# Sixteen parts of unread products of ones, placed in TensorE's order by new tables

## The chip, the cores and the metric

The kernel runs on one core of one Trainium2 chip. A time is the device time of one execution in microseconds; the median of several is compared. The core's engines each play an own queue of instructions in order and meet through semaphores: TensorE (PE, matmuls; its weight loads are PEld), VectorE (DVE), ScalarE (ACT) and GpSimd (POOL). SyncE (SP) starts DMAs. Matmul results stand in eight PSUM banks, the rest in SBUF.

## The reference

Eight batches of eight heads, 576 positions of 64 numbers. The attention is causal by blocks of 64 positions, and its result is the input of a mixing layer of width 512.

```python
scores = q @ k.T / 8, masked where block(key) > block(query)     # blocks of 64
x      = softmax(scores) @ v                       # (8, 576, 512): 8 heads side by side
theta  = x @ w_theta
zr, zi = x * cos(theta), x * sin(theta)
y      = w_tok_r @ zr + w_tok_i @ zi               # over the 576 positions
u      = x + y
out    = u + maximum(u @ w_ch, 0)
```

## The kernel before

The work is cut into 3434 parts, small functions that each issue one to some tens of instructions, mostly on one engine. 64 heads go in 32 pairs (one head in each half of the partitions), eight heads make a batch of the mixing layer.

For a pair, SyncE loads q, k and v. The first pairs use them in f32; later ones are split into a high and a low f16 part (`q_high`, `k_high`, then the lower parts at L581 and L586), with scales from the maxima of the data (L395 spreads them over the partitions by a product with ones, from a diagonal made at L382 on VectorE, L387 on ScalarE or L389 on GpSimd). Scores (L610, mask L617, the first small tile L638) come in wide tiles, which take two banks each (`s_123`, `s_124` in the order), and narrow ones in single banks (`g_125` to `g_128`). VectorE takes row maxima (L658), someone turns them into a bias (L668 or L670), ScalarE makes the exponentials (L674, tiles `t_110`, `t_111`). The first eight heads are transposed by TensorE (L699) and copied out of the banks (L450 ScalarE, L452 VectorE or GpSimd); the others are split into f16 parts (high L450/L452, low L455) and transposed by a DMA (L721). Then come the weighted sums (L732, f32, the first four heads, L741 in f16) and their division by the row sums (L757 to L765).

The mixing layer makes theta (L888, six or nine matmuls a step), its sines (to L931), the products with x (L940), their f16 parts (low L455), the mixing over positions (L964), u = x + y (the copy of x, L969; the sum, L973), its f16 parts, the last product (L987), the rectifying pass (L993 ScalarE, L995 VectorE) and the sum (L1003).

The weights come in raw by DMA (L481) and are rounded and split: an exponent on ScalarE (L490), the lowest bits (L496 ScalarE, L498 GpSimd, L500 VectorE), a narrowing on VectorE (L504), then the plain part (L459 or L520). Their column sizes come from products with ones (L513). Ahead of all, `WARMING = 11` matmuls of 128x512 ones with ones (L363) run while the first data are loaded.

No engine's order follows from the code alone. `emit` plays the parts in the order of a table, and so sets every engine's queue:

```python
for label in parts[key].takes:
    of_label[label] = banks[int(next(names))]          # BANKS: a digit for each label
if parts[key].on:
    place[key] = next(places, parts[key].on[0])        # PLACES: A, D, P or S
...
for n in ORDER:                                        # numbers of parts
    parts[keys[n]].f(*([place[keys[n]]] if parts[keys[n]].on else []))
```

`ORDER` holds each part once, `BANKS` the bank of each tile of results, `PLACES` the engine of each part that several can do (A ScalarE, D VectorE, P GpSimd, S SyncE). The waits follow from what a part reads and writes.

Of the kernel before, what the change touches and what calls it, by code (L numbers as in the profile page):

```python
# [37 lines left out]
WARMING = 11  # L38
WHOLE = 3

ORDER = [
# [214 lines left out]
def attention_phase_mixer(  # L256
# [10 lines left out]
    nc = tc.nc  # L267
# [927 lines left out]
    for b, m in enumerate(mixers):  # L1195
# [45 lines left out]
        for e, th in mixes:  # L1241
# [4 lines left out]
            part("out", (e, th), m.total, [("relu", b, e, th), ("ul", b, e)], leaves=[("c", b, e, th)])  # L1246
        for e in range(NDT):
            part("store", (e,), m.store, [("out", b, e, th) for th in range(2)])

    with tc.manual_schedule():  # L1250
        emit(parts, banks, bank_of)

# [45 lines left out]
```

## Time and profile before

| | us |
|---|---|
| median of 3 runs | 644.75 (644.53 to 645.04) |
| the profiled execution | 644.28 |
| its span | 642.5 |
| TensorE busy | 617.8 |
| VectorE, ScalarE, GpSimd busy | 566.7, 521.1, 358.5 |

The span runs from the first to the last instruction of the profiled execution. In the rows below `DVE`, `ACT`, `POOL`, `PE` name the engines, and `L610` is line 610 of the kernel before. A matmul's busy time is modelled by its end, so starts are the surer numbers.

### The profile page before, as it was taken

To read this page: it belongs to the slowest core of one execution; us is meant where nothing else is said; L and a number is where in the kernel's file an instruction comes from. 1 tells how busy PE (TensorE), PEld (TensorE's weight loads), DVE (VectorE), ACT (ScalarE), POOL (GpSimd) and SP (SyncE) were. 2 spreads that over 40 slices of the span, in tenths; PEclk is the share of its full clock that TensorE was granted. 3 is DMA by queue.
4 is the path that set the end of the run, shared out by engine and by line. 5 is a ranking of instruction groups with operands and counts; after the bars stand their busy time and mean duration, and the time that the engine had idled before them with its cause. 6 is when DMAs were issued, how large, how long until landed. Compare 5 with 4: busy or idle time off the path is not lost.

```text
span 642.5 us, 18107 instructions
## 1 busy us (share of the span) xinstructions
PE 617.8 (96%) x7423; PEld 467.6 (73%) x7425; DVE 566.7 (88%) x1129; ACT 521.1 (81%) x869; POOL 358.5 (56%) x383
## 2 busy tenths in 40 slices
PE   6899989999999999999999999999999999999997
PEld 3778657866886678767878678785876678857775
DVE  5899999888989999999999989899999989777654
ACT  5899899988997999889999999979998998127112
POOL 3436586673744548448695377572656563734340
PEclk8999999999999999999999999999999999999999
DMA  8964998999696797979799996979796647920101
GB/s 321 387 244 134 162 209 175 206 188 245 104 254 134 158 213 179 196 155 193 147 215 181 174 195 184 192 128 238 192 217 134 124 90 137 183 60 2 38 38 74
DMA packets 238772, 109.23 MB, mean 170 GB/s; under 512 B 226017, under 2 KB 226017, under 8 KB 238689
## 3 DMA queue, kind: packets, MB, share of 16 engines
q1 hardware_dynamic: 238688, 108.07, 76.6%
q8 instruction: 58, 0.95, 0.6%
q14 instruction: 26, 0.20, 0.1%
HBM read 42.01 MB, written 9.44 MB: 80 GB/s over the span
## 4 chain that ended last, share of the span: by engine, by line
PE 61%; ACT 18%; DVE 11%; issue 5%; DMA 3%; POOL 2%; SPq 1%; DVEq 0%; ACTq 0%; POOLq 0%
PE g L964 14%; PE s L964 8%; PE g L741 7%; PE g L888 5%; PE s L888 5%; ACT t L674 5%; PE g L987 5%; PE s L610 5%; PE s L987 4%; DVE m L658 3%; ACT aa L931 2%; PE g L610 2%; ACT junk L850 2%; DMA rk<-in_k 1%; ACT rr L929 1%
## 5 line engine op out<-in xcount | busy, mean ns | idle before, releaser
L964 PEld LDWEIGHTS <-zh 128*128 128x128 f16 x1152 | 112.7, 98 | 31.9 <-issue 2.6
L455 POOL TENSOR_TENSOR p<-t,p 128x1536 f16<-128x1536 f32 (+4 forms) x28 | 75.7, 2706 | 72.9 <-ACT p L450 41.1
L964 PE MATMUL g<-wT_h,zh 128*128 128x288 f16 x378 | 108.4, 287 | 0.2 <-DVE rr L906 0.2
L964 PE MATMUL g<-wT_l,zh 128*128 128x288 f16 x378 | 108.2, 286 | 0.0
L964 PE MATMUL g<-wT_h,zl 128*128 128x288 f16 x378 | 108.2, 286 | 0.0
L741 PEld LDWEIGHTS <-pt 128*128 128x128 f16 x2700 | 89.8, 98 | 8.8 <-issue 2.8
L741 PE MATMUL g<-v,pt 128*128 128x65 f16 x2700 | 92.5, 194 | 3.5 <-DVE xn L765 1.3
L658 DVE TENSOR_REDUCE m<-s 128x1 f32<-128x448 f32 (+2 forms) x132 | 85.0, 671 | 5.0 <-PE s L617 4.8
L450 ACT CAST p<-t 128x1536 f16<-128x1536 f32 (+4 forms) x51 | 68.1, 1337 | 0.9
L964 PEld LDWEIGHTS <-zl 128*128 128x128 f16 x576 | 56.3, 98 | 16.0 <-issue 1.5
L888 PEld LDWEIGHTS <-xT 128*128 128x128 f16 x384 | 36.6, 98 | 41.4 <-issue 1.9
L455 DVE TENSOR_TENSOR p<-t,p 128x1600 f16<-128x1600 f32 (+4 forms) x36 | 61.6, 1715 | 4.6 <-ACT p L450 3.9
L674 ACT ACTIVATE t<-s,m,size 128x576 f32<-128x576 f32 (+1 forms) x80 | 60.1, 779 | 6.5 <-DVE m L670 2.5
L658 DVE TENSOR_REDUCE m<-g 128x1 f32<-128x192 f32 (+2 forms) x156 | 54.3, 370 | 7.4 <-PE g L617 7.4
L964 PE MATMUL s<-wT_h,zh 128*128 128x288 f16 x198 | 56.7, 286 | 1.0 <-ACT t L674 1.0
L987 PEld LDWEIGHTS <-wch_h 128*128 128x128 f16 x512 | 48.2, 98 | 12.5 <-issue 0.2
L964 PE MATMUL s<-wT_h,zl 128*128 128x288 f16 x198 | 56.7, 286 | 0.0
L964 PE MATMUL s<-wT_l,zh 128*128 128x288 f16 x198 | 56.7, 286 | 0.0
L674 ACT ACTIVATE t<-g,m,size 128x320 f32<-128x320 f32 (+2 forms) x100 | 50.2, 534 | 1.3 <-POOL m L670 0.8
L940 POOL TENSOR_TENSOR aa<-aa,xn 128x256 f32<-128x256 f32 (+1 forms) x59 | 46.4, 798 | 8.8 <-ACT aa L931 7.0
L987 PE MATMUL g<-uh,wch_h 128*128 128x288 f16 x152 | 43.6, 287 | 0.1
L987 PE MATMUL g<-uh,wch_l 128*128 128x288 f16 x152 | 43.5, 286 | 0.0
(208 smaller groups left out, 1640.9 us busy)
## 6 DMA issues: line engine op xcount, KB each, us to landing
rv<-in_v SPq DMA_DIRECT2D x16, 768.0 KB, 5.8
rq<-in_q SPq DMA_DIRECT2D x15, 640.0 KB, 5.3
out<-xT SPq DMA_DIRECT2D x32, 288.0 KB, 2.6
rk<-in_k SPq DMA_DIRECT2D x15, 576.0 KB, 4.6
w_raw<-in_w_tok SPq DMA_DIRECT2D x5, 576.0 KB, 5.8
pt<-in_w_tok SPq DMA_DIRECT2D x4, 576.0 KB, 9.1
w_raw<-in_w_theta SPq DMA_DIRECT2D x4, 512.0 KB, 7.6
w_raw<-in_w_ch SPq DMA_DIRECT2D x4, 512.0 KB, 4.2
```

What stands on the lines that cost most here:

```text
L450: nc.scalar.copy(out=out, in_=x)
L455: engine_of(on).tensor_tensor(out=out, in0=x, in1=y, op=ALU.subtract)
L610: nc.tensor.matmul(to[hh][:, col:col + n], lhsT=qq[rows, P + P * i:P + P * i + P], rhs=kk[rows, k0:k0 + n], start=nn == 0 and col % 512 == ...
L658: nc.vector.tensor_reduce(out=self.m[:, i:i + 1], in_=self.scores_of(i), axis=AX.X, op=ALU.max)
L674: nc.scalar.activation(out=t_parts[self.hh][:, to:to + n], in_=self.scores_of(i), func=AF.Exp, scale=self.scales()[0], bias=self.m[:, NI + ...
L741: nc.tensor.matmul(o[:, i, :], lhsT=source[:, block, :], rhs=vv[:, slot, hh, :], start=first, stop=last)
L850: nc.scalar.activation(out=junk[:, 0:PG * n].rearrange("p (g c) -> p g c", g=PG), in_=x, func=AF.Abs, accum_out=self.scales_of(what, g).su ...
L888: nc.tensor.matmul(g, lhsT=xT[:, xx + i, :], rhs=ww[:, dt, :], start=first, stop=last)
L931: nc.scalar.activation(out=to, in_=x, func=AF.Sin, scale=-2.0 * math.pi, bias=half_pi[rows])
L940: engine_of(on).tensor_tensor(out=cd, in0=cd, in1=self.xns[dt][:, i0:i0 + ni, :], op=ALU.mult)
L964: nc.tensor.matmul(g, lhsT=zz[:, kk, cols], rhs=ww[:, kk, ts], start=(n == 0 and kk == k0 and nn == 0), stop=n == 4 and kk == k0 + ni - 1 ...
L987: nc.tensor.matmul(g[:, 0:HS], lhsT=ww[:, dt, e * P:(e + 1) * P], rhs=uu[:, dt, th * HS:(th + 1) * HS], start=dt == 0 and n == 0, stop=dt ...
```

## The change

`FILLS = 16` new parts are added, 3450 in all. Each is two matmuls of 128x512 of the tile `ones` with itself into a bank that the tables name; no instruction reads the result. They come in order of their number. All three tables are new: the order of all parts, the bank of all tiles, the engine of all parts with a choice. No other function is changed. Lines of the kernel after stand two lower down to the new function (L363 becomes L365).

```diff
+FILLS = 16
...
 ORDER = [
-    157, 154, 0, 16, 8, 32, 40, 324, 155, 352, 323, 328, 158, 1, 353, 24, 329, 2, 340, 360, 325, 327, 351, 361, 9, 17,
...
 BANKS = (
-    "6516655545201236420123455012346501235420123650123100123540123640123540123460123560123560123560123450123540123540"
+    "6536423445101236520123455012346501235410123650123100123540123640123540123460123560123560123560123450123540123540"
...
+    def fill(n):
+
+        for _ in range(2):
+            nc.tensor.matmul(bank_of["f", n], lhsT=ones, rhs=ones.unsqueeze(1).broadcast_to([P, 4, P]), start=True, stop=True)
+
+    for n in range(FILLS):
+        add(("fill", n), step_of(fill, n), [("fill", n - 1) for _ in range(n > 0)], takes=[("f", n)])
```

TensorE at the front, from the mask of the first wide scores on. Before, with transposes of the first narrow exponentials (`t_111`) and then the second pair's narrow scores:

```order
L617 LDWEIGHTS mask_q
L617 MATMUL s_124<-ones,mask_q 128x2x64
L638 MATMUL g_128<-rk,rq 128x64
L699 MATMUL g_125<-ident_r,t_111 128x128 x4
L610 MATMUL g_125<-rk,rq 128x320
L610 MATMUL g_126<-rk,rq 128x320
```

And after:

```order
L619 MATMUL s_124<-ones,mask_q 128x2x64
L1255 LDWEIGHTS ones
L1255 MATMUL g_125<-ones 128x512
L1255 LDWEIGHTS ones
L1255 MATMUL g_125<-ones 128x512
L701 MATMUL g_126<-ident_r,t_111 128x128 x4
L701 MATMUL g_127<-ident_r,t_110 128x128 x4
L612 MATMUL g_125<-rk,rq 128x320
```

Fill 0 stands behind the first wide scores, and the transposes of both heads (`t_111`, `t_110`) ahead of the second pair's scores; before, those of `t_110` stood behind them.

VectorE at the front, from its third instruction on. Before, row maxima of the first narrow scores come first:

```order
L321 CAST ident_r<-made_ident 128x128
L658 TENSOR_REDUCE m<-g_125 128x1
L658 TENSOR_REDUCE m<-g_127 128x1
L658 TENSOR_REDUCE m<-g_125 128x1
L658 TENSOR_REDUCE m<-g_127 128x1
L670 TENSOR_SCALAR m<-m 128x2
```

And after:

```order
L323 CAST ident_r<-made_ident 128x128
L506 SCALAR_TENSOR_TENSOR w_val<-w_val,w_raw 128x512
L502 TENSOR_SCALAR w_raw<-w_raw 128x512
L660 TENSOR_REDUCE m<-g_127 128x1
L660 TENSOR_REDUCE m<-g_126 128x1 x2
L660 TENSOR_REDUCE m<-g_127 128x1
```

A narrowing and the lowest bits of two pieces of theta stand ahead of the same four maxima. On SyncE the start of the first piece of theta stands ahead of those of the first q and k, which were the first two before.

TensorE among the transposes ahead of the narrow scores that started at 50 us before (`t_110`, `t_111` are exponentials, `g` and `s` banks). Before:

```order
L732 MATMUL g_128<-qk_103,pt_120 128x65 x15
L699 MATMUL s_123<-ident_r,t_110 128x128 x8
L699 MATMUL g_126<-ident_r,t_110 128x128
L699 MATMUL s_124<-ident_r,t_111 128x128 x8
L610 MATMUL g_126<-rk,rq 128x320
```

And after:

```order
L701 MATMUL s_123<-ident_r,t_110 128x128 x8
L1255 LDWEIGHTS ones
L1255 MATMUL g_126<-ones 128x512
L1255 LDWEIGHTS ones
L1255 MATMUL g_126<-ones 128x512
L701 MATMUL g_126<-ident_r,t_110 128x128
L701 MATMUL s_124<-ident_r,t_111 128x128 x8
L1255 LDWEIGHTS ones
L1255 MATMUL g_125<-ones 128x512
```

Fills 5 and 6 stand between the same transposes, and fill 7 follows a few rows on. The places of all: 0 and 1 ahead of the second wide scores, 2 to 4 from there to the third, 5 to 7 here, 8 ahead of narrow scores that ran at 88 us before, 9 to 13 in one row ahead of a weighted sum (L743) and 14 and 15 ahead of scores, both between 89 and 106 us.

On the other engines: VectorE makes 21 copies of x (L969) in place of 14, GpSimd 11 in place of 18. VectorE makes the low part of 10 tiles of 1536 exponentials (L455) in place of 7, GpSimd 14 in place of 17. VectorE makes 10 low parts of 512 cosines in place of 15, 25 products of `rr` (L940) in place of 31. Half of a head's copy to the other partitions (`other_half`) is a DMA 5 times in place of 14.

## Rows read from the trace of the kernel before

**Rows 1.** The page: busy time, share and instructions; granted clock in 40 slices.

```profile
PE 617.8 (96%) x7423; PEld 467.6 (73%) x7425; DVE 566.7 (88%) x1129; ACT 521.1 (81%) x869; POOL 358.5 (56%) x383
...
PEclk8999999999999999999999999999999999999999
```

**Rows 2.** Stretches: us from:to, length, busy us (and instructions) of each engine, clock, DMA.

```profile
5.60:23.57 17.97, 11.46 (x79) 8.53 (x80) 13.86 (x30) 13.93 (x27) 5.06 (x8) 0.81 1.00 394
23.57:41.45 17.88, 16.03 (x137) 14.23 (x138) 17.24 (x42) 16.59 (x29) 6.42 (x9) 1.00 0.79 296
41.45:88.98 47.53, 47.19 (x547) 36.28 (x547) 45.95 (x102) 42.41 (x83) 31.01 (x40) 1.00 0.74 175
88.98:106.40 17.42, 13.47 (x202) 10.27 (x203) 16.60 (x38) 16.94 (x29) 12.62 (x16) 1.00 0.87 185
106.40:134.00 27.60, 27.60 (x371) 22.71 (x368) 25.35 (x61) 26.62 (x51) 18.83 (x19) 1.00 1.04 196
...
141.60:527.30 385.70, 380.04 (x4891) 283.88 (x4888) 359.99 (x703) 353.69 (x570) 230.87 (x219) 1.00 0.85 177
527.30:638.40 111.10, 111.08 (x1109) 85.80 (x1108) 79.10 (x144) 43.70 (x74) 43.96 (x40) 1.00 0.38 77
```

**Rows 3.** TensorE's timeline: start, us, line, tiles, and in brackets the wait before.

```profile
12.63 1.12 PE L699 MATMUL g<-ident_r,t 128*128 128x128 f32 x4 [3.40 <-ACT t L674]
15.12 2.18 PE L610 MATMUL g<-rk,rq 64*128 64x320 f32 x12 [1.38 <-DMA rk<-in_k]
...
23.57 2.19 PE L610 MATMUL s<-rk,rq 64*128 64x512 f32 x14 [0.63 <-DVE pt L452]
```

**Rows 4.** The front on VectorE and ScalarE, the same columns.

```profile
6.90 1.42 DVE L658 TENSOR_REDUCE m<-g 128x1 f32<-128x320 f32 x4 [4.48 <-PE g L617]
...
8.11 0.67 ACT L490 ACTIVATE w_val<-w_raw 128x512 f32<-128x512 f32 x1 [6.10 <-DMA w_raw<-in_w_theta]
...
10.63 1.22 ACT L490 ACTIVATE w_val<-w_raw 128x512 f32<-128x512 f32 x2 [0.80 <-DMA w_raw<-in_w_theta]
```

**Rows 5.** The front's stretch at half clock, columns as in rows 2.

```profile
12.11:18.94 6.83, 4.93 (x26) 4.03 (x27) 5.25 (x13) 6.11 (x14) 2.55 (x5) 0.50 1.03 411
```

**Rows 6.** The chain of waits from 67 to 84: start, us, what.

```profile
71.42 1.94 PE g L888 x9
```

**Rows 7.** TensorE's timeline between 89 and 106 us.

```profile
96.31 1.52 PE L741 MATMUL g<-v,pt 128*128 128x65 f16 x45 [1.07 <-DVE xn L765]
```

**Rows 8.** TensorE's timeline at 140 us.

```profile
140.08 1.54 PE L741 MATMUL g<-v,pt 128*128 128x65 f16 x45 [1.18 <-DMA pt<-p]
```

**Rows 9.** TensorE's waits (total, times, longest); GpSimd and ScalarE ahead of 337 us.

```profile
PE g L395 <- ACT diag L387: 1.5, 2, 1.2
...
332.33 2.36 POOL L670 TENSOR_SCALAR m<-m,size 128x4 f32<-128x4 f32 x1 [0.31 <-DVE m L658]
...
334.73 0.83 ACT L674 ACTIVATE t<-s,m,size 128x576 f32<-128x576 f32 x1 [1.28 <-POOL m L670]
```

**Rows 10.** VectorE, GpSimd and TensorE around 268 us.

```profile
267.38 0.88 DVE L581 SCALAR_TENSOR_TENSOR qk<-rq,size,qk 128x640 f16<-128x640 f32 x1
...
268.24 1.77 DVE L586 SCALAR_TENSOR_TENSOR qk<-rk,size,qk 128x576 f16<-128x576 f32 x1
...
268.24 1.16 POOL L455 TENSOR_TENSOR zl<-rr,zh 128x512 f16<-128x512 f32 x1 [6.57 <-ACT zh L450]
...
270.06 0.57 PE L610 MATMUL g<-qk 64*128 64x320 f16 x14 [0.71 <-DVE qk L586]
```

**Rows 11.** Groups of moved operations: ns min/median/max, first and last start, forms.

```profile
L969 DVE TENSOR_TENSOR u<-xT x14: 741/750/1062, 117.7 to 603.4; 128x576 f32<-128x576 f16 x14
...
L455 DVE TENSOR_TENSOR p<-t,p x36: 723/1814/2353, 73.2 to 543.5; 128x1600 f16<-128x1600 f32 x22, 128x1536 f16<-128x1536 f32 x7, 128x1088 f16<-128x1088 f32 x3, 128x1024 f16<-128x1024 f32 x2
...
L455 DVE TENSOR_TENSOR zl<-aa,zh x23: 377/683/1295, 107.3 to 613.9; 128x512 f16<-128x512 f32 x15, 128x256 f16<-128x256 f32 x8
...
L940 DVE TENSOR_TENSOR rr<-rr,xn x31: 407/414/1370, 97.9 to 594.3; 128x256 f32<-128x256 f32 x31
```

More of the change, by code (lines that the diff above doesn't have):

```diff
@@ L38 @@
 WARMING = 11
+FILLS = 16
 WHOLE = 3
 ORDER = [
[173 rows of a table removed]
[174 rows of a table added]
 ]
 BANKS = (
-    "6516655545201236420123455012346501235420123650123100123540123640123540123460123560123560123560123450123540123540"
-    "1235401234601235401234601234601234501235401235601235601234601235601236501234601236401236501236534651065144560654"
-    "1125654103440466660156605051421066635545056616452065051046560146656415211404405544431542045244560645564643410045"
-    "136253346021506432021451634504146250135"
+    "6536423445101236520123455012346501235410123650123100123540123640123540123460123560123560123560123450123540123540"
+    "1235401234601235401234601234601234501235401235601235601234601235601236501234601236401236501236524650065144564354"
+    "0145654215640066654166665051421064635545056616402565051046560146656405210414415544451642045266540645564644410425"
+    "0652633065310524101254664325461042631354262254446666666"
@@ L221 @@
 )
 PLACES = (
-    "ADPPDPPDPPDPPAPDAPPAPPAPPAPDAPPAPDAAPAADAPPAAPAAAAADPAAAAAAPADDPDDSDADADPADAAPDASPADADSAPADPAAPPAPAAPPPAAAADPPAP"
-    "ADAADDDDAPDADAPAAPDAAAPPPAPAPAPDPPPAPPPADPADDAPADPAPAAAPADPADDPAAPPAPDAAAADDSAAPAPAAADDPDDPAADPADDAPADAPPAADDAPA"
-    "PAAAPAPADASPAPDPAAAPADDPAAPADAPAPADDPAAPAPDPPADDASDADDAAAAPDDDSAAPDAAAPDDDDSPAPDPDAPAADAPPPDDSPPDAADAPPADAAAAAAA"
-    "DASDAPDPAAADADDPAAPAAAAPAADDSAAPDSPDPAADASPADADAAAAADDPPAPDAAPAAADDAAAPDPAAPPDDDAPPPDPAPAAADASPADDAAAADADDDAAPDP"
-    "AAAPDPDAPAPDDPAPPAPASAADAAPPADADAPPDPDPPPPPPPAPDADADPPAPDDADPDADPDAPDDADDDAPDPAPPPADDDADDPAPDAPDPAPDAADADDAAADAP"
@@ L228 @@
-    "DPAPDDAADPDAPPDAPPPADPPADPPADPPADDDPDPPADPDADPPDDDPDPDADAADADADDAAPAPAPADAADADDDPDDPAPPDADPPPPPPAPPPAPDPAPPPAPDP"
-    "ADDDDDPAPAPPDAAAAAAADAAPPPAPAPDDAADPPAPDPAPDPPPDPAPPPAPPDAPPPAPPPAPPPAPDPAPPPDAPADPDAAADDDDADPDADAPDDAAAPPDPPPPD"
-    "DPDPPDAPPDPPDPAPPPAPPPPPPDAPPDPPPADADADDDDADAAADPDADAPPPAADDDPPPDPPPPDDPPPDADDPPDDDPPDDADDDAPDDAPPPAPDAPPPADAAAA"
-    "DADAAADAPAPPDDDDDAPPADDDDDPPDDDDADPPADPPADDPPDDDADPPDDPPPDPAPDPAPAAAADAADAADAPADDDDADDDDDAPDPAPPDDDPPDDPPPDDDPDD"
-    "DAPDDADDPPDDDDPPAPPDPPAAAAAAAAA"
+    "DDPPAPADPPDPPAAPAPPAPPAPDAPPAAPAPPAPAAAPAAPDAPAAPAADPAAAAAADPDDPDDSPAPAAPPPDAPDAPPAPDDDAAADPAAPPAPADPPPAAPADADAA"
@@ new lines @@
+    "ADAAPDDPAPDADAPAAPDAAAPPAAPDPAPDPPPDAPPADPADAAPADPAPDPAAADPADDPPAPAAPAAAPADAADAPDDAAADAPDDPAPPAADADPADDDAAADDAAP"
+    "DDAPAAAADASDAPDSAPAAADDPAAPAPADADADDAAAPAAPPADDDDADADAAAAAAADDAAAPASAAAPDDAADAPAPPDAPADAADPDAAPPAAADAPPADDADAADA"
+    "DDDAAPDPAAAAADAPDPDDAAAPPADDDAAPDAPAPPADASAADDAAAAPADDSPAPDDAAPAADDPDAPDPAPPDDDDPPDPAAAAAAADDPAADDAAAAPADDAPAPDP"
+    "AADPDPAPPADDPPAAAAPDAAAPAPPPPPADDDAADADPPPPAPAPDADADPPAPDDADPDADPPAPPPADDDAPDDAPDDADPDAPPDADDADPDADPAADDAAAAADAP"
+    "APAPDDADADDAPPPDPPDDPDPAPDPPPPPADPPPDPPAPPPADPPAPDPDAPDPPDDAAADDDDPDPPPDDAADDDPPAPDPAPPDAPPDPPPPDPPPAPPDPDPDAPPD"
@@ L233 @@
+    "APDPADPPDAPPDAAAAAAAAAAPPPADDDDADDDPPAPDPADPDDPPPAPPDADPPADDPAPPPAPPDADPDAPPPPADPDAADADDAAAPDADAPAPAADADPPPDPPPD"
+    "PDDPPDPDPPPDPDAPDPAPPPAPDPAPPPAPPADAPADADDAAAAADAPADADAPAADDDPPPDPPPPPPADPDAPDDPDDDAPDPADPDAPDDAPDPAPDAPAPADAADD"
+    "DAADAADAPAPDDDDDDAPDADPPPDPPAPPPPDDPAPPPAPDDDDPDAPDPPDPDDPDADPDPDADADDDAAAAPPDPDDPADADADPPDPPDDDPPPDPAPPPAPPDADP"
+    "DPDPPDPPPPDPPDDPADADPDPDADDADAA"
 )
```

346 rows, old and new, of the table ORDER are left out of this document.

## Prediction

> **What bounds the kernel now.** I read the page first: TensorE is busy 617.8 of 642.5 us and granted the full clock in almost every slice [rows 1]. The busy time in nine stretches then shows where its 24.7 us of idle time lie [rows 2]: 6.51 from 5.60 to 23.57, 1.85 up to 41.45, 0.34 up to 88.98, 3.95 up to 106.40, none up to 134, 5.66 from 141.6 to 527.3, 0.02 behind that up to 638.4; the rest, 6.4, is the start, one wait of 1.18 for a DMA at 140 [rows 8] and the tail behind the last matmul. So up to 41 us and around 90 to 106 the other engines set the pace (VectorE and ScalarE busy 16.60 and 16.94 of 17.42), and elsewhere TensorE does, with VectorE close behind (359.99 of 385.70). The timelines of those places name the waits: at the front scores and transposes wait for exponentials, for the second k and for a copy out of a bank [rows 3]; at 96 us weighted sums wait for VectorE [rows 7].
>
> **The fills.** A fill is two matmuls of 128x512, with a weight load each. A step of nine 16-bit matmuls of that width in the chain of waits takes 1.94 us, 0.2156 each [rows 6]; a fill is 0.431, sixteen 6.90. A matmul that hides wholly in a wait costs nothing, one on a busy TensorE its full time. By their place in the order, fills 0 and 1 (0.86) stand ahead of the second wide scores, in the stretch with 6.51 of idle time; 2 to 4 (1.29) in the one with 1.85; 5 to 8 (1.73) in the one with 0.34; 9 to 15 (3.02) in the one with 3.95. The first, second and fourth lots fit. The third does not: 47.19 + 1.73 = 48.92 against a stretch of 47.53, **+1.39** (0 if the new order has waits there that the old one has not, 1.73 at most). No fill stands where TensorE idles 5.66 us in 141.6 to 527.3.
>
> In the row the spacing is 215.6 ns. The Trainium skill (TensorE: Matmul & The Clock Gate, Back-to-back issue gap) gives some 131 ns for a sustained matmul of that width and 216 for an isolated one. By 131 the third lot would be 1.05 and overfill its stretch by 0.71 instead of 1.39; this row agrees with the larger figure.
>
> **The front (0 to 41.45).** SyncE now starts a third of theta ahead of q and k. Before, q and k were in when the warm-up ended, and the first VectorE maxima ran at 6.90; the first theta was in at 8.11 [rows 4]. As third of the transfers the last of q and k comes between 5.6 and 8.1. On VectorE the first four maxima now stand behind a narrowing of theta and the lowest bits of the next one. That transfer is in between 8.11 and 10.63, the two ends of ScalarE's waits for theta [rows 4]; I take 9.4, add ScalarE's 0.67 and as much on VectorE, and the maxima begin near 10.7, not 6.90. They take 1.42; two exponentials later the first transposes start at about 13.1, against 12.63 [rows 3]. This loses little because before the same exponentials stood behind the weights on ScalarE (a wait to 10.63). The second scores wait for k until 15.12 as before, since the same bytes are ahead of it; now both heads' first transposes lie before that wait and fill 1.38 us of it. ScalarE's list up to the last wide exponential ends at about 19.2 against 19.4, and the copies out of the banks, one of which held the second wide scores for 0.63 [rows 3], are spread anew, so most of that wait goes: −0.2 −0.45 = **−0.65** at 41.45. Bounds: −1.6 (the 1.38 filled in full besides) and +1.0 (theta in at 10.6).
>
> **89 to 141.6.** Lateness at 88.98 is −0.65 + 1.39 = +0.74. From 89 to 106 3.95 of idle time, less 3.02 of fills, leave 0.93 for it, unless VectorE, which has 0.82 to spare, is late too; what is left meets the wait of 1.18 for a DMA of turned exponentials [rows 8], which a rounding pass releases and TensorE does not. So **−0.74**, and TensorE is level at 141.6. Bound: nothing is absorbed, 0.
>
> **141.6 to 527.3.** Two effects. First, at 337 us TensorE waits 1.2 us for a diagonal of sizes on ScalarE that stood behind two exponentials, which waited for a bias on GpSimd; that pass took 2.36 us for 128x4 elements [rows 9]. In the new order ScalarE makes the diagonals ahead of these exponentials, so the wait goes: **−1.2** (0 if the next wait is right behind it). Second, the tables give VectorE more: 21 residual copies instead of 14 (+7 x 0.750 = 5.25), 10 roundings of 1536 instead of 7 (+3 x 1.814 = 5.44), against 5 fewer low parts of cosines (−5 x 0.683 = −3.42) and 6 fewer products (−6 x 0.414 = −2.48) [rows 11]: +4.8; smaller moves go both ways. VectorE had 25.7 us idle here, but not everywhere: before the scores at 270 TensorE already waited 0.71 for its low part of k [rows 10], and now a normalising pass and a product stand in that chain, some 0.4 each (the product by [rows 11]), with TensorE's work ahead of these scores unchanged. I take +0.8 there and once more for all later pairs, whose sizes and low parts stand behind more VectorE work too, **+1.6**; bounds 0 (all in idle time) and +4.8 (all on the path).
>
> That passes stretch beside each other shows at 268 us: a low part took 1.77 us on VectorE, with GpSimd busy too, against the 0.88 of the one before it [rows 10]. The Trainium skill (SBUF, Who interferes with whom) says that a VectorE instruction with two SBUF inputs contends with a GpSimd one that reads SBUF, and whoever issues first holds the shared port. By it, what leaves GpSimd also unblocks VectorE, and part of the +4.8 would be given back; the sum does not use it. The 2.36 us pass agrees with it.
>
> **527 to the end.** TensorE is busy 111.08 of 111.10 and does the same matmuls; the order of a few does not matter. 0.
>
> **The sum.** −0.65 + 1.39 − 0.74 − 1.2 + 1.6 = +0.4: span 642.5 + 0.4 = 642.9. The profiled execution took 644.28, 1.78 outside its span, and the median of the runs is 644.75, 0.47 above it: 642.9 + 1.78 + 0.47 = **645.1**. A measurement of this kernel tells some 0.2% (1.29 us) from no change, so faster means under 643.46, slower over 646.04.
>
> **Rivals.**
> Faster, the fills keep the clock. TensorE idled from 9.22 to 12.63 [rows 3] and was granted half the clock from 12.11 to 18.94, with 4.93 us busy in it [rows 5]: at the full clock 2.46 less. Fill 0 stands in that idle stretch. Against it: it is 0.43 of 3.4, and q and k come later, so a new idle stretch opens ahead of the first scores. Were the clock kept, the part behind k's arrival (about 1.0) would come off the front, the extra VectorE work would stay in idle time (0 instead of +1.6) and the front's earlier start carry through: −1.65 + 1.39 − 1.2 and nothing to absorb, −1.5, or down to −3.7 if fills 5 to 8 fall into waits as well. 643.3 to 641.0, middle 642.3. It wins if VectorE's load never reaches a score. Chance 0.35.
> Slower, VectorE becomes the bound between 141.6 and 527.3. It was busy 93% there, and +4.8 lifts that to 94.6%. It decides from the point where the low part of k, at the scores near 270 and behind, ends later than TensorE's last work ahead of it; then each operation inserted is paid in full: +3.6 to +4.8 in place of +1.6, with the lateness of 0.74 kept: 647.8, up to 649.1. For it: the 0.71 wait there now. Against it: a mean of 21 us still idle. Chance 0.20.
> Slower, the front. If VectorE's lowest bits wait for theta until 10.63 or more, the maxima begin at 12 and first transposes end behind k's arrival: each us is passed on to 41.45, where no idle time takes it before 89 us. +1.0 instead of −0.65: 646.5. Chance 0.08.
> That the fills do nothing is the forecast itself: its sum has no clock gain in it. Chance of the forecast 0.37.
>
> **How the numbers follow.** The forecast is 645.1, the likeliest. The range goes to the faster rival's far end, 641.0, and short of the slower one's, 648.6, leaving out about 0.1 on each side. Faster 0.35, same 0.37, slower 0.28.
>
> **What would show it.** For the fills: sixteen pairs of matmuls of ones, those between 47 and 51 us without a wait ahead of them, and the 41 to 89 stretch longer by about 1.4 while the 89 to 106 one is shorter. For the front: first maxima near 10.7, second wide scores near 22.9. For the clock: whether the 6.83 us at half clock are there still. For the middle: no wait at the diagonal near 337, and waits for low parts of k near 270 grown. The forecast is wrong if the stretch from 141.6 on changes by more than 2 us, or the half-clock stretch moves to another, busier place.

## The result and the profile after

| | median, us | range | profiled execution | its span |
|---|---|---|---|---|
| before | 644.49 | 643.49 to 646.76 | 644.28 | 642.5 |
| after | 639.36 | 639.08 to 643.14 | 639.16 | 637.3 |

The changed kernel is faster: ratio 0.9919, 95% interval 0.9899 to 0.9940, some 5.2 us. The forecast was 645.1, no change, and the range, 641.0 to 648.6, does not hold the time.

The page of the kernel after, its busy time and its granted clock in 40 slices:

```profile
PE 622.2 (98%) x7457; PEld 467.4 (73%) x7457; DVE 570.1 (89%) x1131; ACT 517.9 (81%) x870; POOL 354.2 (56%) x389
...
PEclk9999999999999999999999999999999999999999
```

Against [rows 1] TensorE is 4.4 us busier. The fills are 6.9 of that, an estimate by the spacing of [rows 6]; so its other work takes some 2.5 less, with a shorter warm-up (3.98 us against 4.62) and less work at half clock at the front (2.94 us against 4.93). Its idle time falls from 24.7 us (642.5 less 617.8) to 15.1, by 9.6, but most of that is filled and not gained: with the fills it is 22.0. So of the 5.2 us some 2.7 are shorter waits and some 2.5 shorter work.

The stretches of the kernel after (columns as in [rows 2]), cut at the same work: the wide scores of pairs 1, 2, 6 and 9, which began at 23.57, 41.45, 89.88 and 133.98 before, and of pair 31 (527.35 before):

```profile
0.00:21.54 21.54, 15.91 (x94) 9.66 (x95) 14.14 (x28) 14.73 (x25) 9.45 (x45) 0.92 0.91 356
21.54:39.80 18.26, 17.55 (x143) 14.91 (x143) 17.67 (x39) 17.02 (x30) 11.32 (x16) 1.00 0.89 341
39.80:88.52 48.72, 48.51 (x557) 35.90 (x556) 46.84 (x106) 43.76 (x87) 28.28 (x33) 1.00 0.74 176
88.52:106.00 17.48, 16.68 (x224) 12.13 (x225) 16.86 (x37) 17.23 (x30) 13.42 (x18) 1.00 0.77 153
106.00:132.73 26.73, 26.73 (x359) 21.85 (x358) 25.85 (x62) 26.17 (x50) 13.54 (x15) 1.00 1.12 203
132.73:141.60 8.87, 8.87 (x100) 5.55 (x99) 8.41 (x18) 7.06 (x14) 8.28 (x5) 1.00 0.95 177
141.60:521.62 380.02, 376.52 (x4880) 281.79 (x4880) 360.60 (x707) 352.19 (x576) 220.69 (x210) 1.00 0.86 178
521.62:634.00 112.38, 111.46 (x1109) 85.61 (x1108) 79.42 (x140) 39.69 (x66) 49.22 (x52) 1.00 0.37 76
```

The lead over the kernel before is 2.03 us at pair 1, 1.65 at pair 2, 1.36 at pair 6, 1.25 at pair 9, 5.73 at pair 31 and 5.09 at the last matmul. So the front gives some 1.7 in these two executions, the fills up to 133 us cost little, and the rest comes behind: from pair 9 on idle time falls by 3.15 us (1.18 + 5.66 + 0.02 before, 3.50 + 0.21 now; 0.71 of the last row is the tail), and TensorE is 0.7 us less busy with the same matmuls (4977 up to pair 31 and 1109 behind it, in both traces). What shortened these is not shown.

The front of the kernel after on TensorE, then on VectorE, and its stretch at half clock:

```profile
6.24 1.20 PE L612 MATMUL g<-rk,rq 64*128 64x320 f32 x12 [1.20 <-DMA rk<-in_k]
...
11.57 0.66 PE L701 MATMUL g<-ident_r,t 128*128 128x128 f32 x4 [1.02 <-ACT t L676]
...
13.93 1.93 PE L612 MATMUL g<-rk,rq 64*128 64x320 f32 x12 [0.37 <-DMA rk<-in_k]
```

```profile
8.21 0.43 DVE L502 TENSOR_SCALAR w_raw<-w_raw 128x512 uint32<-128x512 uint32 x1 [2.30 <-DMA w_raw<-in_w_theta]
8.55 1.41 DVE L660 TENSOR_REDUCE m<-g 128x1 f32<-128x320 f32 x4
```

```profile
14.24:17.65 3.41, 2.94 (x20) 2.37 (x17) 2.78 (x6) 2.79 (x6) 1.39 (x3) 0.50 1.03 417
```

q and k come later, as expected (scores at 6.24, not 5.60), but the first maxima begin at 8.55, not at 10.7, the first transposes at 11.57 against 12.63 [rows 3], and 3.41 us are at half clock instead of 6.83 [rows 5].

The fills between 92 and 98 us, on TensorE's timeline of the kernel after, and two places where waits of the kernel before are gone:

```profile
92.53 2.32 PE L1255 MATMUL g<-ones 128*128 128x512 bf16 x10
95.18 1.51 PE L743 MATMUL g<-v,pt 128*128 128x65 f16 x45 [0.33 <-DVE xn L767]
96.53 1.02 PE L1255 MATMUL g<-ones 128*128 128x512 bf16 x4
97.88 2.40 PE L612 MATMUL s<-rk,rq 64*128 64x512 f32 x13 [0.32 <-ACT t L676]
...
137.53 1.53 PE L743 MATMUL g<-v,pt 128*128 128x65 f16 x45
...
332.05 0.32 PE L397 MATMUL g<-diag,ones 128*128 128x384 bf16 x1 [0.20 <-ACT diag L389]
```

The fills stand in one long wait and one shorter one, of which 0.33 and 0.32 are left. The 1.18 us for the DMA at 140 [rows 8] are gone, those of 1.2 for the diagonal [rows 9] are 0.20.

TensorE's waits between pair 9 and pair 31 (total, times, longest), before and then after, by what ended them:

```profile
PE g L395 <- ACT diag L387: 1.5, 2, 1.2
PE s L888 <- ACT t L674: 1.2, 1, 1.2
PE g L741 <- DMA pt<-p: 1.2, 1, 1.2
PE g L610 <- DVE qk L586: 0.7, 1, 0.7
PE s L964 <- ACT t L674: 0.7, 1, 0.7
PE s L395 <- ACT diag L387: 0.4, 1, 0.4
...
```

```profile
PE g L743 <- DMA pt<-p: 1.8, 2, 0.9
PE g L640 <- DVE qk L583: 0.8, 1, 0.8
PE s L612 <- ACT t L676: 0.3, 1, 0.3
PE g L397 <- ACT diag L389: 0.2, 1, 0.2
PE s L966 <- ACT t L676: 0.2, 1, 0.2
```

The waits for ScalarE fall from 3.8 us to 0.7, those for VectorE from 1.6 (four shorter ones of 0.2 to 0.3 included) to 0.8, and those for DMAs rise from 1.2 to 1.8.

### The profile page after: what moved, and what is told of

Read it like the earlier page. It is cut to its first block, busy times and chain, and to the rows that moved or that the text cites. A ratio compares the mean times of both kernels' runs of the same rounds, so it can differ in the third digit from the quotient of the medians.

```text
span 637.3 us, 18146 instructions
## 1 busy us (share of the span) xinstructions
PE 622.2 (98%) x7457; PEld 467.4 (73%) x7457; DVE 570.1 (89%) x1131; ACT 517.9 (81%) x870; POOL 354.2 (56%) x389
## 4 chain that ended last, share of the span: by engine, by line
PE 71%; ACT 11%; DVE 7%; DMA 6%; issue 3%; POOL 1%; SPq 1%; DVEq 0%; ACTq 0%
PE g L966 18%; PE g L743 10%; PE s L966 9%; PE g L989 7%; PE g L890 6%; PE s L612 5%; PE s L989 5%; PE s L890 4%; DMA pt<-p 4%; ACT t L676 3%; PE g L612 2%; ACT junk L852 2%; DMA w_raw<-in_w_theta 2%; DVE m L660 1%; ACT p L452 1%
## 5 line engine op out<-in xcount | busy, mean ns | idle before, releaser
L457 POOL TENSOR_TENSOR p<-t,p 128x1536 f16<-128x1536 f32 (+4 forms) x25 | 65.7, 2631 | 88.3 <-ACT p L452 61.1
L743 PEld LDWEIGHTS <-pt 128*128 128x128 f16 x2700 | 89.6, 98 | 8.2 <-DMA pt<-p 3.1
L743 PE MATMUL g<-v,pt 128*128 128x65 f16 x2700 | 92.7, 193 | 2.4 <-DMA pt<-p 1.8
L660 DVE TENSOR_REDUCE m<-s 128x1 f32<-128x576 f32 (+3 forms) x132 | 84.9, 671 | 2.6 <-PE s L619 2.2
L452 ACT CAST p<-t 128x1600 f16<-128x1600 f32 (+4 forms) x51 | 68.1, 1341 | 3.2 <-DMA pt<-p 2.5
L457 DVE TENSOR_TENSOR p<-t,p 128x1600 f16<-128x1600 f32 (+4 forms) x39 | 67.1, 1721 | 3.0 <-ACT p L452 2.3
L942 POOL TENSOR_TENSOR aa<-aa,xn 128x256 f32<-128x256 f32 (+1 forms) x65 | 50.3, 787 | 20.3 <-ACT aa L933 16.6
L660 DVE TENSOR_REDUCE m<-g 128x1 f32<-128x320 f32 (+2 forms) x156 | 53.7, 370 | 1.3 <-PE g L619 0.6
L966 PE MATMUL s<-wT_h,zh 128*128 128x288 f16 x189 | 54.0, 286 | 0.4 <-ACT t L676 0.4
L966 PE MATMUL s<-wT_l,zh 128*128 128x288 f16 x189 | 54.0, 286 | 0.0
L457 POOL TENSOR_TENSOR zl<-aa,zh 128x512 f16<-128x512 f32 (+1 forms) x31 | 36.9, 1197 | 26.8 <-ACT zh L452 23.6
L989 PE MATMUL g<-uh,wch_h 128*128 128x288 f16 x164 | 47.0, 286 | 0.0
```

What stands on the lines that cost most here:

```text
L452: nc.scalar.copy(out=out, in_=x)
L457: engine_of(on).tensor_tensor(out=out, in0=x, in1=y, op=ALU.subtract)
L660: nc.vector.tensor_reduce(out=self.m[:, i:i + 1], in_=self.scores_of(i), axis=AX.X, op=ALU.max)
L743: nc.tensor.matmul(o[:, i, :], lhsT=source[:, block, :], rhs=vv[:, slot, hh, :], start=first, stop=last)
L942: engine_of(on).tensor_tensor(out=cd, in0=cd, in1=self.xns[dt][:, i0:i0 + ni, :], op=ALU.mult)
L966: nc.tensor.matmul(g, lhsT=zz[:, kk, cols], rhs=ww[:, kk, ts], start=(n == 0 and kk == k0 and nn == 0), stop=n == 4 and kk == k0 + ni - 1 ...
```

## The experiments

| kernel | median | before beside it | ratio |
|---|---|---|---|
| no_fills | 641.52 | 644.24 | 0.9951 |
| fills_0_1 | 641.13 | 644.24 | 0.9949 |
| fills_2_to_15 | 639.52 | 644.24 | 0.9924 |
| fills_9_to_13 | 638.96 | 643.92 | 0.9925 |
| fills_9_to_15 | 638.59 | 643.79 | 0.9920 |
| before_with_fills | 647.00 | 644.24 | 1.0041 |
| before_fills_9_to_15 | 643.54 | 644.35 | 0.9990 |
| new_front_old_rest | 643.16 | 643.79 | 0.9994 |
| old_front_new_rest | 640.34 | 643.79 | 0.9941 |
| maxima_first | 639.22 | 644.35 | 0.9931 |
| sizes_first | 644.11 | 643.79 | 1.0005 |
| old_copies_of_x | 643.11 | 643.92 | 0.9998 |
| old_low_parts | 644.97 | 643.92 | 1.0018 |
| old_copies | 649.55 | 644.35 | 1.0096 |
| old_engines | 694.79 | 644.35 | 1.0788 |

Executions of one kernel differ by 1 to 3 us at the front, with the time at which the first data come and the clock falls; the kernel before began its second wide scores at 23.57 in the execution shown and at 22.55 in that of sizes_first, whose front is the same. So differences of medians below 0.5 us are not read here. The kernel before itself measures 643.79 to 644.35 from group to group, so kernels of different groups are compared by their ratios to it as well. The time from the third wide scores (pair 2) to the last matmul leaves the front out; in the executions shown it is 596.6 us in the kernel before, 595.6 in no_fills, 596.0 in fills_0_1, 593.6 in fills_2_to_15, 593.2 in the kernel after, 592.7 in fills_9_to_13 and 592.6 in fills_9_to_15.

**Which fills matter.** The tables stay, and the fills issue only for some numbers (none, `n < 2`, or `n >= 2` as here):

```diff
-        for _ in range(2):
+        for _ in range(2 if n >= 2 else 0):
```

> The changed kernel with its three tables as they are, and all sixteen fills issue nothing. Theory A, the gain is the work of the new order and engines, and fills cost what TensorE has no wait for: fills 5 to 8 (1.73 us) stand in a stretch with 0.22 us of idle time left, so without them 1.0 to 1.7 us less than the changed kernel: 637.7 to 638.4; the half clock at the front stays as short (some 3 us). Theory B, the fills keep TensorE's clock: without them the half-clock stretch grows back to some 6.8 us and the time rises to 641 or more.

> The changed kernel with only fills 0 and 1, those of the first 21 us. Theory A: as without any fill, 637.7 to 638.4. Theory B: only these two can bear on the clock at the front, so 639.4 or less, with the half-clock stretch as short as in the changed kernel, and clearly under the kernel without fills.

> The changed kernel without fills 0 and 1. Theory A: 639.4, no difference, since both stood in waits. Theory B: 641 or more, with a half-clock stretch of some 6.8 us at the front.

Neither theory held as written. Without fills the time rises by 2.2, so they are worth something, against theory A (the tables alone are worth the other 2.7, 641.52 against 644.24); but fills 0 and 1, the only ones at the front, bring 0.4 of it at most, and leaving them out alone changes nothing, against theory B's place. The stretches of no_fills between 90 and 106 us show where (columns as in [rows 2]; the seventh number, behind the busy times, is the granted clock), and TensorE's timeline there:

```profile
90.00:94.00 4.00, 2.40 (x57) 2.12 (x54) 4.00 (x12) 3.90 (x7) 3.82 (x6) 1.00 0.30 60
94.00:98.00 4.00, 1.92 (x46) 1.79 (x46) 4.00 (x9) 3.98 (x7) 3.68 (x6) 0.93 1.04 193
98.00:102.00 4.00, 4.00 (x17) 3.15 (x18) 2.55 (x6) 4.00 (x9) 1.62 (x3) 0.50 0.32 118
102.00:106.00 4.00, 4.00 (x65) 3.86 (x63) 2.81 (x6) 2.67 (x7) 3.11 (x5) 0.72 1.00 188
```

```profile
94.89 1.51 PE L743 MATMUL g<-v,pt 128*128 128x65 f16 x45 [2.49 <-DVE xn L767]
97.59 4.51 PE L612 MATMUL s<-rk,rq 64*128 64x512 f32 x14 [1.19 <-ACT t L676]
```

The new order does the weighted sums of one head and the first small scores without a wait and then waits 2.49 us for VectorE, where the kernel before waited in pieces of 0.2 to 1.1, here the first two:

```profile
89.88 2.17 PE L610 MATMUL s<-rk,rq 64*128 64x512 f32 x16 [0.91 <-DVE rr L906]
...
93.70 1.53 PE L741 MATMUL g<-v,pt 128*128 128x65 f16 x45 [1.01 <-DVE m L658]
```

Behind that wait, and within the next of 1.19, the clock granted to TensorE, which was busy 4.3 of the 8 us from 90 to 98, falls from 2.4 GHz to 1.2, from 97.41 to 104.24, while scores stand on it without a wait. In fills_0_1, which has the same wait of 2.49, it falls within that wait. The two stretches at half clock, no_fills first:

```profile
97.41:104.24 6.83, 6.65 (x31) 5.79 (x32) 4.43 (x9) 5.52 (x14) 4.45 (x6) 0.50 0.61 154
```

```profile
94.06:104.31 10.25, 9.43 (x77) 8.09 (x76) 7.75 (x16) 8.90 (x18) 7.42 (x11) 0.50 0.77 166
```

The scores of pair 8 begin 2.2 us later in no_fills than in the changed kernel (123.15 against 120.92), where the clock is full from 88 to 142 us.

**The two late waits alone.** The same edit with `n >= 9`, then `9 <= n < 14`:

> The changed kernel with fills 9 to 15 only, those between 92 and 98 us. Theory C, drawn from the runs without fills, whose granted clock was half from 94 or 97 to 104 us: these seven alone hold the clock in a wait that the new order has gathered in one place, and the others at best cost nothing. Then 638.4 to 639.5, with the full clock from 90 to 110 us. Rival: fills 2 to 8 pace the work ahead as well; then clearly above 639.5, towards the 641.1 of the kernel with fills 0 and 1 only.

> The changed kernel with fills 9 to 13 only, the five that fill the wait of 2.5 us at 92 us; 14 and 15 fill one of 1.2 at 96. If the first wait alone lets the clock fall, the time stays at 638.4 to 638.7 with the full clock from 90 to 110; if both have to be filled, it rises in some or all executions towards 641.

Theory C held. With fills 9 to 15 alone the time is 638.59, the lowest median here, 0.8 to 0.9 under those of the kernels that also have fills 2 to 8. By their ratios (0.9920 against 0.9919 and 0.9924) the three can't be told apart; by the times from pair 2 on, 0.6 and 1.0 us lie between them in the executions shown. Their stretches there, for comparison:

```profile
94.00:98.00 4.00, 3.34 (x53) 1.98 (x51) 3.97 (x10) 3.98 (x8) 3.68 (x6) 1.00 0.96 177
98.00:102.00 4.00, 4.00 (x56) 3.33 (x55) 3.60 (x8) 4.00 (x9) 1.62 (x3) 1.00 0.46 153
102.00:106.00 4.00, 3.85 (x52) 3.13 (x49) 3.81 (x12) 3.87 (x10) 4.00 (x5) 1.00 1.16 167
```

TensorE's 56 matmuls in 98 to 102 stand against 17 at half clock. Fills 14 and 15 are not needed: without them the clock is full and the time the same within 0.4.

**Fills in the old order.** The kernel before with the parts of the fills put into its `ORDER`, each ahead of the same neighbour on TensorE, and free banks for them:

```diff
-    3, 341, 10, 11, 56, 362, 363, 33, 162, 326, 41, 34, 350, 48, 330, 364, 372, 18, 160, 331, 342, 332, 12, 354, 355,
+    3, 341, 10, 11, 56, 362, 3434, 363, 33, 162, 326, 41, 34, 350, 48, 330, 364, 372, 18, 160, 331, 342, 332, 12, 354,
```

> The kernel before, its order, banks and engines untouched, with the sixteen fills put ahead of the same parts of TensorE's work as in the changed kernel, into banks that are free there. Theory A: 644.5 plus the part of fills 5 to 8 that finds no wait, 1.4: 645.9. Theory B: the clock at the front is kept, 642.5 or less. If fills shift TensorE's pace in a useful way whatever the order, also under 644.

> The kernel before with the seven fills 9 to 15 alone, between 93 and 98 us, its tables untouched. There TensorE's idle time comes in four pieces of 0.4 to 1.1 us and the granted clock is full without fills. Theory C: nothing to keep, so nothing gained: 643.8 to 644.6 (0 to 0.8 dearer, where they don't fit in the waits). Rival: fills help there whatever the order: under 643.

All sixteen cost 2.8 us there, the seven late ones nothing (ratio 0.9990, 0.9979 to 1.0000). So fills gain nothing by themselves: they keep the clock through a wait that the new order gathers, and where the clock is full without them they cost what does not fit.

**Front and rest.** One kernel's parts up to the second pair's wide scores, with their banks and engines, then the rest of the other's (the start of new_front_old_rest is shown; old_front_new_rest has fills 2 to 15):

```diff
-    157, 154, 0, 16, 8, 32, 40, 324, 155, 352, 323, 328, 158, 1, 353, 24, 329, 2, 340, 360, 325, 327, 351, 361, 9, 17,
+    8, 154, 157, 0, 16, 32, 40, 9, 155, 10, 324, 158, 11, 24, 12, 56, 1, 2, 325, 17, 328, 353, 352, 18, 329, 360, 323,
...
```

> The kernel before, but its parts up to the second pair's wide scores come in the changed kernel's order, with its engines and banks, and no fills. Theory D, the front's gain of 2.0 us at these scores carries to the end: 644.3 - 2.0 = 642.3. Rival: VectorE and ScalarE, which set the pace up to 106 us, take it back: 643.5 to 644.3.

> The other half: the parts up to the second pair's wide scores as in the kernel before, the rest in the changed kernel's order with its engines and banks and with fills 2 to 15. Theory D: 639.5 + 2.0 = 641.5. Rival: the front's gain is given back later anyway: 639.5 to 640.

By the medians the new front is worth 0.6 with the old rest, which is not clear of noise (ratio 0.9994, 0.9983 to 1.0005), and 0.8 with the new one (640.34 against 639.52; 1.1 by the ratios 0.9941 and 0.9924): not 2.0, and close to the −0.65 of the prediction. In the executions shown of the five kernels with the old front the third wide scores begin at 39.94 to 41.45, median 40.70; in those of the eleven with the new front as it is, at 39.66 to 43.90, median 39.80. The rest, with fills 2 to 15, is worth 3.5 without its front (0.9941, 0.9929 to 0.9954).

The length of the half-clock stretch at the front does not follow the fills: it is 6.82 us (8.08 to 14.90) in the execution shown of fills_2_to_15 and 3.41 (12.51 to 15.92) in that of fills_9_to_15, both without fills 0 and 1, and in that of no_fills the clock is full up to 90 us.

The pass that gated the maxima, put behind them, with the exponentials ahead of two weight passes (based on fills_9_to_15):

```diff
-    8, 154, 157, 0, 16, 32, 40, 9, 155, 10, 324, 158, 11, 24, 12, 56, 1, 2, 325, 17, 328, 353, 352, 18, 329, 360, 323,
+    8, 154, 157, 0, 16, 32, 40, 9, 155, 10, 324, 158, 11, 24, 12, 56, 1, 325, 328, 353, 352, 329, 360, 323, 2, 3, 361,
...
```

> As fills_9_to_15, but the first four maxima stand ahead of the lowest bits of theta on VectorE (that pass waited for its DMA until 8.21 and the maxima began at 8.55), and the first exponentials ahead of two weight passes on ScalarE. If that pass gates the front: maxima from 7.5, first transposes near 10 instead of 11.6, and 0.3 to 1.0 less at the second wide scores and at the end: 637.6 to 638.3. Rival: the second scores wait for k until 13.9 in any case and the weights come later: 638.6 or a little more.

The rival held: the maxima begin at 7.51, but the second wide scores at 21.78 against 21.65, and the time is no lower (0.6 more by the medians, with overlapping intervals of the ratios). The gate of the maxima is not what the front's end waits for.

**The wait for the diagonal alone.** In the kernel before the maximum of sizes and the diagonals (parts 265 and 266) move ahead of the two exponentials:

```diff
-    2517, 1241, 264, 1230, 2511, 2494, 1242, 1244, 265, 2523, 1188, 2547, 2525, 2512, 2513, 2502, 2526, 266, 267,
+    2517, 1241, 264, 1230, 265, 266, 2511, 2494, 1242, 1244, 2523, 1188, 2547, 2525, 2512, 2513, 2502, 2526, 267,
```

> The kernel before with one move: at 333 us the maximum of sizes (L793) comes right behind the low part it stood two operations behind, and the diagonals (L387) ahead of the two exponentials that wait for GpSimd's bias. The prediction's step: TensorE's wait of 1.2 us near 337 goes, and the time falls by 1.2 to 643.1. Rival: another wait takes its place right behind, within 0.3 of the kernel before.

No gain (1.0005, 0.9994 to 1.0016). ScalarE's and TensorE's timelines of sizes_first:

```profile
334.14 0.99 ACT L387 ACTIVATE diag<-ident_r,size 128x128 bf16<-128x128 f32 x3 [1.29 <-DVE size L793]
```

```profile
342.40 0.23 PE L638 MATMUL g<-qk 128*128 128x64 f16 x2 [1.05 <-DVE qk L581]
```

The diagonals come earlier and TensorE no longer waits 1.2 us for them, but at 342 it waits 1.05 for a low part of q. VectorE was as late as ScalarE.

**VectorE's added work.** Engines of single parts go back to those of the kernel before, the order stays (based on fills_9_to_15). One row of the table for the copies of x, the others alike:

```diff
-    "APDPADPPDAPPDAAAAAAAAAAPPPADDDDADDDPPAPDPADPDDPPPAPPDADPPADDPAPPPAPPDADPDAPPPPADPDAADADDAAAPDADAPAPAADADPPPDPPPD"
+    "APDPADPPPAPPDAAAAAAAAAAPPPADDDDADDDPPAPDPADPDDPPPAPPDADPPADDPAPPPAPPDADPDAPPPDAPPDAADADDAAAPDADAPAPAADADPPPDPPPD"
```

> As fills_9_to_15, but the copies of x (L971) and the low parts of exponentials (L457) back on the engines of the kernel before, 20 parts; nothing else moves. These carry most of the +4.8 us of VectorE's work. The prediction's step: up to 1.6 less, 637.0 to 638. Theory E: no difference. Theory F: 639 or more, since GpSimd takes nearly twice as long for each.

> As fills_9_to_15, with only the copies of x (L971), 15 parts, back on the engines of the kernel before. Both kinds together cost 11 us. Theory G, a pass with two SBUF inputs on GpSimd stretches VectorE's passes beside it, the more the longer it is: the copies (1.3 us each on GpSimd, 11 moved there and 4 away) cost less than half, 640 to 643. Theory H, the cost is each part's later end in an order made for the faster engine: most of the 11 us, as 15 of the 20 parts are these.

> As fills_9_to_15, with only the low parts of exponentials (L457), 5 parts, 4 to GpSimd and 1 away, back on the engines of the kernel before. Theory G: each of the four takes 3.1 us or more on GpSimd and stretches what VectorE does beside it by more than the 1.8 us it gave away (a low part of q took 3.62 instead of 0.84 beside one): 643 to 647, the larger share. Theory H: the smaller share, under 642.

> The changed kernel's order and banks with fills 9 to 15 only (638.6), but behind the second pair's wide scores all 380 parts whose engine the change altered are back on the engine of the kernel before. The prediction's step (VectorE's added work costs TensorE 1.6 us): 637.0. Theory E, the added work is hidden and the gain is the order's alone: within 0.5 of 638.6. Theory F, order and engines only work together: 641 or more, with new waits for VectorE, ScalarE and GpSimd.

Taking VectorE's added passes away costs 11.0 us (649.55 against 638.59): 4.5 by the copies (15 parts, 11 of them to GpSimd), 6.4 by the low parts (5 parts, 4 to GpSimd), which add up. The prediction's step would have gained 1.6. All 380 engines back cost 56 us, growing by some 1.5 us from pair to pair. Busy times of fills_9_to_15 and then of old_copies:

```profile
PE 619.3 (97%) x7437; PEld 466.8 (73%) x7439; DVE 569.0 (89%) x1131; ACT 518.0 (81%) x870; POOL 352.8 (55%) x389
```

```profile
PE 619.8 (96%) x7437; PEld 466.5 (72%) x7439; DVE 576.2 (89%) x1121; ACT 517.6 (80%) x870; POOL 369.7 (57%) x399
```

VectorE does ten passes fewer and is busy 7.2 us longer. Its low parts (L457) and copies of x (L971) take 6.5 us less in old_copies; four kinds of pass whose number is the same (L583, L596, L942, L982, each with at least two tiles read) take 116.5 us instead of 106.0. The same place on VectorE in fills_9_to_15, and on VectorE and GpSimd in old_copies, shows one such stretch:

```profile
367.98 0.84 DVE L583 SCALAR_TENSOR_TENSOR qk<-rq,size,qk 128x640 f16<-128x640 f32 x1
...
369.47 1.75 DVE L457 TENSOR_TENSOR p<-t,p 128x1536 f16<-128x1536 f32 x1
```

```profile
373.52 3.62 DVE L583 SCALAR_TENSOR_TENSOR qk<-rq,size,qk 128x640 f16<-128x640 f32 x1
```

```profile
372.69 3.77 POOL L457 TENSOR_TENSOR p<-t,p 128x1536 f16<-128x1536 f32 x1
```

A low part that took VectorE 1.75 us takes GpSimd 3.77, and VectorE's low part of q, which starts beside it, 3.62 instead of 0.84: it ends 0.7 us behind the other. VectorE gave away 1.75 and lost 2.78. The Trainium skill (SBUF, Who interferes with whom) says that a VectorE instruction with two SBUF inputs contends with a GpSimd one that reads SBUF, and that the order of issue decides which of them blocks; this place agrees with it (GpSimd's pass starts at 372.69, VectorE's at 373.52). What part of the 11 us is such stretching and what part the later end of the moved pass is not separated, since old_low_parts differs in both from its base, and no run moves these passes in the order of the kernel before. Theory G (the low parts cost the larger share) and F (orders and engines belong together) held.

## Why the prediction was wrong

- **The front, −0.65: right in size.** The two halves put it at 0.4 to 1.1, by medians and ratios. Its steps were not all right. The maxima began at 8.55, not at 10.7: the lowest bits are taken from the raw data, so L502 waited for its DMA alone, which was in by 8.21 where I took 9.4, and I had added ScalarE's 0.67 and a pass of its own length. That did not matter, as maxima_first shows. In the two profiled executions the difference is 1.65, since the one of the kernel before had the latest front of its five.
- **Fills 5 to 8, +1.39: too much.** From pair 2 to pair 6 TensorE took 48.72 us with them and 48.22 without (fills_9_to_15): 0.5. In the old order the term held, 50.02 (before_with_fills) against 48.43. The new order has some idle time between 21 and 88 us that the old one has not (without fills, 2.40 us up to pair 2 and 0.86 up to pair 3, against 1.85 and 0.28), as the lower bound allowed.
- **Fills 9 to 15, nothing: right for the time they take, wrong for what they do.** They fit: 0.80 us of idle time is left between 88.5 and 106. But the forecast took them as bare, because it read the clock of the kernel before, which was full there, and not the waits of the new order. The order listing showed the weighted sums of one head moved ahead of the small scores; that a wait gathers there was to be asked. The mechanism was among the rivals, but at the front, where fill 0 is worth nothing that can be measured. Reckoned as in [rows 5], half of the 6.65 us that TensorE was busy at half clock in no_fills bounds the price at 3.3 us; the scores of pair 8 came 2.2 later.
- **The wait of 1.18 at 140 us, +0 after lateness: wrong by about 1.2.** It was to absorb lateness. TensorE was not late, and the new order has the DMA there in time (137.53 has no wait).
- **The diagonal, −1.2: right as a wait, wrong as a gain by itself.** It is 0.20 us now. sizes_first shows that the bound of 0 was the truth for the single move: the next wait, for VectorE, was as late. The sum also put TensorE's other waits for ScalarE at nothing without a reason: 2.55 us of them, at 405, 472, 484 and 495 us, are gone too.
- **VectorE's added work, +1.6: the wrong sign.** This is the step that failed. I put +0.8 on the scores near 270 and as much behind them. No scores wait there now (the 0.71 of [rows 10] are gone), and TensorE's waits for VectorE between pair 9 and pair 31 fell from 1.6 us to 0.8. The +4.8 counted passes of the whole kernel as if they stood between 141.6 and 527.3. Of the seven more copies of x on VectorE two stand ahead of pair 9 and six behind pair 31, where TensorE has no wait to speak of; between these marks there is one fewer (11 in place of 12). VectorE's busy time there rose by 1.9 us (367.14 to 369.01) and GpSimd's fell by 8.9 (237.91 to 228.97). I also priced each pass by the median of its kind and left the engine it came from at nothing: VectorE's low parts of k, 20 in both kernels, take 17.25 us there instead of 19.63. The sentence on the shared port stood beside the sum, with the right direction; the slower rival built on the same +4.8 fell with it.

The sum by the traces: −1.65 for the front, +0.4 from there to pair 9, −3.15 of idle time behind it and −0.7 of busy time with the same matmuls: −5.1 at the last matmul. So the sum missed most from pair 9 on, where it had +0.4 with the DMA's wait left as it was; that is the sign it named for being wrong, more than 2 us behind 141.6. About 0.8 of the front's share is the late front of the one execution; by the medians of all executions shown it is 0.9. The low end of the range, too, was not worked out: the faster rival's −3.7 does not follow from its terms, which give −2.85 (−1.46 less the 1.39 of the fills).

What stays open: which moves of the order made the waits at 270, 472 and 495 us go. The wait at 270 also went in new_front_old_rest, whose order there is that of the kernel before and whose TensorE came 2.2 us later, so VectorE's end there does not seem to hang on TensorE. No run took these moves one by one.

## What to carry to other kernels

A part's engine is not priced by its duration there: ask what runs beside it on the engine it leaves and the one it joins, since VectorE's passes beside a long two-input pass on GpSimd can grow by more than that pass took there. Count the moved parts in the stretch where the price would be paid, not over the whole kernel. When an order is new, read its waits before you judge its fillers; a few unread matmuls are worth their place where waits gather and the clock would fall (here 2.6 us by five of sixteen, 638.96 against 641.52), and cost where TensorE is busy. Taking out one wait of an engine that is busy nearly all the time gains only when the next engine is not as late (sizes_first).

## What the runs showed of the hardware

With one wait of 2.49 us and one of 1.19 within 5.2 us TensorE was granted 1.2 GHz for 6.83 us (no_fills, 97.41 to 104.24), and in fills_0_1 for 10.25 from within its wait of 2.49, while idle time of 3.95 us in pieces of 0.2 to 1.1 over 17 us left it at 2.4 GHz in the kernel before [rows 2]. Filling the wait of 2.49 kept the clock full (fills_9_to_13). And VectorE with ten passes fewer was busy 7.2 us longer (old_copies against fills_9_to_15).
